# Clustered attention with a mixture of experts: a planner that lets VectorE and GpSimd exclude each other, selection's small operands in PSUM, and more experts in plain float32

## The chip, the cores and the metric

The kernel runs on one core of a Trainium2 chip. A core has five engines that work through their own queues of instructions, in order: PE (TensorE, the matmuls; its weight loads are listed apart as PEld), DVE (VectorE), ACT (ScalarE), POOL (GpSimd) and SP (SyncE, which here only issues transfers). SBUF is the working memory of 128 partitions, PSUM the small memory that matmuls write into. The metric is the time of one execution on the device, in microseconds (us); of several runs the median is given.

## The reference

Attention first, for 4 batches, 8 heads, 768 positions and 64 dimensions. Queries and keys are each assigned to the nearest of 16 centroids of their head, by cosine; a query only sees keys of its own cluster.

```python
q_assign = argmax(q_n @ c_n.T); k_assign = argmax(k_n @ c_n.T)
scores = where(q_assign == k_assign, q @ k.T / 8, -1e9)
attn = softmax(scores); x = (attn @ v)          # laid out as 3072 tokens of 512
```

Then a mixture of 8 experts over these 3072 tokens. Each token goes to its best expert; of an expert's tokens only the 80 with the highest gate are kept, the rows of all others are zero.

```python
e = argmax(x @ w_gate); g = softmax(x @ w_gate)[e]
for each expert: keep = the 80 tokens of it with the highest g
out[keep] = g[keep] * (relu(x[keep] @ w1[e]) @ w2[e])   # w1 512x1024, w2 1024x512
```

Everything is float32, and the clusters, the routing and the 80 kept tokens hang on exact comparisons, so the kernel computes to nearly full float32 precision.

## The kernel before

**One planned stream.** The whole program is laid out by a planner in the kernel's own Python. Work is written as lanes: generators that yield a `Step(engine, microseconds, ...)` ahead of the instructions of each step. `Flow.run` keeps a clock for each engine, takes the lanes' next steps, works out when each could start (its needs done, its buffer free, its engine free), picks the engine that can start first, and among its ready steps the one with the smallest due time `at`. The step's instructions are then emitted, and so stand in that order in the engine's queue. `CFG` holds the due times. So a step's cost, its due time or a new rule in `Flow.run` moves instructions on all engines; the data's dependencies stay guarded by semaphores whatever the order. For `alt` steps the planner also chooses between two engines.

**Attention** runs head by head, each in 6 blocks of 128 keys. Per block PE makes the scores (L562, L565, into `st`), ACT takes two exponentials (L584, L586: `pp` in float32 and `hh` in float16), POOL forms their difference `ll` (L593), and PE multiplies both parts with the values, which are split in a high and a low part (L601, `av`). For one block in five the float32 exponential stays in PSUM (`st`), and DVE forms `ll` instead. DVE also takes the row maxima of a first pass (L528 on PE, L530 on DVE) and normalises (L626 to L635). The tokens `x` are written to `xs` in HBM.

**The tail of attention** carries early work of the mixture. `early` starts in the last batch: 8 chunks of 512 KB of w1 (experts 0 and 1) are loaded into `raw` buffers, DVE takes their sums of squares (`stats`, L915), and `digits` cuts the gates `G` of the first 18 of 24 token tiles into digits: per level a shift (`di`, L694), a comparison with a ramp that gives `ge` (L696), a second shift (`pi`, L700) and a product with the routing one-hot `OH` that gives `pre` (L701); both results lie in the buffer `dug`. Up to now `di` and `pi` are in SBUF.

**Selection** finds each expert's 80th highest gate, digit by digit from the top, in five levels. In `select`, a level counts on PE how many candidates have a digit of at least each value (L747, into `q`), DVE compares the counts with what remains to be chosen (L781, `j`, `nf`), PE adds the chosen digit to the prefix in `nb` (L740), and DVE marks the candidates that still share the prefix (L790, `alive`). `digits` supplies the last batch's 6 tiles between. Then the threshold `thr`, the masks `M`, a scan `C` (L807), the slot of each kept token, and the row numbers `gi` (L850).

**The mixture** runs expert by expert on 80 tokens. POOL's queue gathers the rows (L1048) and scatters the results (L1172). ACT takes the rows' sums of squares, DVE makes a power of two of them (`power`, L878 to L881) and splits the scaled tokens in two float16 parts (L1065, L1066), PE turns them (L1085), and the hidden layer is 32 x 3 = 96 products of split tokens and split weights (L1114). A w1 chunk is split by ACT or DVE (high part, L1011 to L1016) and by DVE or POOL (low part, L1023, L1025). ReLU is ACT's, its low part `hl` DVE's (L1130). An expert in `native2` has its w2 multiplied as it was loaded, in plain float32: 8 products instead of 24 (L1142). The others' w2 is split in two parts on ACT or DVE (L1035, L1037) and POOL or DVE (L1041). An expert in `native1` would have its tokens and w1 multiplied in plain float32, 32 products instead of 96, without sums of squares, powers or splits. A raw chunk's buffer comes free once it is split; a plain one's when its products are done.

## Time and profile before

| | |
|---|---|
| median of 3 runs | 627.25 us (627.02 to 629.78) |
| the profiled execution | 624.93 us |
| its span, first to last instruction | 623.2 us |
| mean granted TensorE clock | 0.938 |
| busy in the span: PE / DVE / ACT / POOL | 552.7 / 501.1 / 474.4 / 441.3 us |
| moved | 114.26 MB |

The span covers everything from the first to the last instruction; 1.73 us lie around it. A row of a group gives line, engine, operation, tiles and shapes, the count after an x, then busy time, mean ns of one, and idle time of the engine just before it with what ended it. A row in order of time gives start and duration in us. A wait inside an instruction, as for a port, counts as its busy time. In the trace a float32 product shows as two weight loads and two matmuls. Line numbers are those of the kernel before.

### The profile page before, as it was taken

The page shows a single profiled execution, that of the slowest core. Times are in us where ns is not written, and L with a number is a line of the kernel's source. Part 1 is how long each engine was busy: PE and PEld are TensorE (multiplying, and loading weights), DVE is VectorE, ACT ScalarE, POOL GpSimd, SP SyncE. Part 2 cuts the span into 40 slices and gives each one's busy share as a digit, 9 for nine tenths or more (in the row PEclk, how much of TensorE's full clock was granted, in tenths as well). Part 3 has the DMA queues.
Part 4 walks back from the last instruction along what each step waited for, and adds up shares of the span by engine and source line. Part 5 has one row for each costly group of instructions (what it writes and reads, how often), then busy time and mean ns, then how long its engine had stood idle before and what let it go on. Part 6 is the DMA issues. An engine that isn't in the chain of part 4 may idle for free.

```text
span 623.2 us, 17162 instructions
## 1 busy us (share of the span) xinstructions
PE 552.7 (89%) x6781; PEld 448.7 (72%) x6781; DVE 501.1 (80%) x1070; ACT 474.4 (76%) x773; POOL 441.3 (71%) x276
## 2 busy tenths in 40 slices
PE   8999999999999999999999999998673638879795
PEld 7567877888888878888788888987562537565373
DVE  4868877888888888878878788799659848987992
ACT  7788788899899799889888987885449239746760
POOL 5359758799968689977688997776449215774775
PEclk9989999999999999999999999999775559989989
DMA  8688975499975489896448556492033773698200
GB/s 301 170 238 221 261 195 126 111 223 287 258 211 135 121 194 259 243 300 154 126 114 207 129 138 157 138 377 82 0 117 146 237 257 124 205 323 309 102 16 22
DMA packets 69776, 114.26 MB, mean 183 GB/s; under 512 B 7072, under 2 KB 38464, under 8 KB 69696
## 3 DMA queue, kind: packets, MB, share of 16 engines
q1 hardware_dynamic: 68672, 110.54, 61.7%
q0 software_dynamic: 1024, 2.62, 1.3%
q8 instruction: 54, 0.88, 0.6%
q14 instruction: 26, 0.21, 0.1%
HBM read 60.46 MB, written 13.89 MB: 119 GB/s over the span
## 4 chain that ended last, share of the span: by engine, by line
PE 53%; DVE 20%; DMA 9%; issue 6%; ACT 5%; POOL 5%; SPq 1%; POOLq 0%; ACTq 0%; DVEq 0%
PE av L601 15%; PE sm L528 11%; PE st L562 9%; PE st L565 8%; DMA raw<-in_w_dram 3%; DVE mx L530 2%; DVE w1p L1025 2%; DVE room L915 2%; POOL w1p L1023 2%; DVE dug L696 1%; PE misc L211 1%; ACT hh L586 1%; PE hp L1114 1%; DMA KAB<-hi 1%; DVE dug L701 1%
## 5 line engine op out<-in xcount | busy, mean ns | idle before, releaser
L593 POOL TENSOR_TENSOR ll<-pp,hh 128x768 f16<-128x768 f32 x154 | 255.1, 1669 | 78.0 <-ACT hh L586 38.9
L530 DVE TENSOR_REDUCE mx<-sm 128x1 f32<-128x384 f32 x384 | 201.7, 551 | 46.8 <-PE sm L528 44.2
L584 ACT ACTIVATE pp<-st 128x768 f32<-128x768 f32 x154 | 124.9, 811 | 42.3 <-PE st L565 37.8
L528 PE MATMUL sm<-KAB,QAB 80*128 80x384 f32 x384 | 141.3, 394 | 1.7 <-DVE mx L530 1.1
L601 PEld LDWEIGHTS <-hh 128*128 128x128 f16 x2304 | 121.8, 99 | 25.7 <-issue 15.1
L601 PE MATMUL av<-vh,ll 128*128 128x73 f16 x1152 | 135.6, 198 | 3.1 <-POOL ll L593 3.1
L601 PE MATMUL av<-vh,hh 128*128 128x73 f16 x1152 | 137.9, 200 | 0.0
L601 PE MATMUL av<-vl,hh 128*128 128x72 f16 x1152 | 136.7, 198 | 0.0
L586 ACT ACTIVATE hh<-st 128x768 f16<-128x768 f32 x154 | 124.6, 809 | 0.0
L601 PEld LDWEIGHTS <-ll 128*128 128x128 f16 x1152 | 113.5, 99 | 3.6 <-POOL ll L593 3.6
L562 PE MATMUL st<-QAB,KAB 128*128 128x384 f32 x384 | 105.2, 355 | 6.7 <-DVE ll L593 5.3
L565 PE MATMUL st<-QAB,KAB 81*128 81x384 f32 x384 | 100.5, 343 | 0.5 <-DMA QAB<-row 0.5
L528 PEld LDWEIGHTS sm<-KAB,QAB 80*128 80x128 f32 x384 | 70.1, 189 | 22.1 <-DVE mx L530 12.4
L562 PEld LDWEIGHTS st<-QAB,KAB 128*128 128x128 f32 x384 | 67.4, 193 | 12.0 <-DVE ll L593 5.2
L565 PEld LDWEIGHTS st<-QAB,KAB 81*128 81x128 f32 x384 | 71.1, 192 | 0.8 <-DMA QAB<-row 0.8
L1114 PE MATMUL hp<-xt,w1p 128*128 128x80 f16 x768 | 33.7, 213 | 6.2 <-POOL w1p L1023 6.1
L1048 POOL DMA_INDIRECT room<-xs,gi x8 | 16.2, 2020 | 31.7 <-DVE g L855 15.3
L593 DVE TENSOR_TENSOR ll<-st,hh 128x768 f16<-128x768 f32 x38 | 36.1, 949 | 2.6 <-ACT st L586 2.5
L1114 PEld LDWEIGHTS <-w1p 128*128 128x128 f16 x768 | 32.6, 108 | 7.5 <-POOL w1p L1023 6.5
L318 POOL TENSOR_TENSOR vl<-ldv,vh 128x512 f16<-128x512 f32 x24 | 27.1, 1128 | 11.6 <-ACT vh L316 11.6
L584 ACT ACTIVATE hh<-st 128x768 f16<-128x768 f32 x38 | 31.0, 817 | 4.2 <-PE st L565 3.9
L1023 POOL TENSOR_TENSOR w1p<-raw,w1p 128x1024 f16<-128x1024 f32 x12 | 27.8, 2332 | 5.0 <-ACT w1p L1012 4.9
(282 smaller groups left out, 988.0 us busy)
## 6 DMA issues: line engine op xcount, KB each, us to landing
raw<-in_w_dram SPq DMA_DIRECT2D x38, 512.0 KB
KAB<-hi SPq DMA_DIRECT2D x60, 192.0 KB
QAB<-hi SPq DMA_DIRECT2D x30, 384.0 KB
room<-in_w_dram SPq DMA_DIRECT2D x22, 512.0 KB
ldk<-in_kT_dram SPq DMA_DIRECT2D x16, 384.0 KB
ldq<-in_qT_dram SPq DMA_DIRECT2D x16, 384.0 KB
ldvt<-in_vT_dram SPq DMA_DIRECT2D x12, 512.0 KB
ldv<-in_v_dram SPq DMA_DIRECT2D x12, 512.0 KB
```

What stands on the lines that cost most here:

```text
L318: nc.gpsimd.tensor_tensor(lo, t[:, c], hi, op=ALU.subtract)
L528: nc.tensor.matmul(s, lhsT=qj, rhs=k[0:D + C, 0, f * HS:(f + 1) * HS], start=True, stop=True)
L530: nc.vector.tensor_reduce(mx[:, j, f:f + 1], s, axis=AX.X, op=ALU.max)
L562: nc.tensor.matmul(s[:, f, 0:HS], lhsT=k[:, 1, ks], rhs=q[:, 1, qs], start=True, stop=False)
L565: nc.tensor.matmul(s[:, f, 0:HS], lhsT=k[0:D + C + 1, 0, ks], rhs=q[0:D + C + 1, 0, qs], start=False, stop=True)
L584: nc.scalar.activation(order[0], s, AF.Exp, scale=float(D) ** -0.5)
L586: nc.scalar.activation(order[1], s, AF.Exp, scale=float(D) ** -0.5)
L593: eng.tensor_tensor(ll, pp, hh, op=ALU.subtract)
L601: mm = lambda out, l, r, **kw: nc.tensor.matmul(out, lhsT=l, rhs=r, skip_group_check=True, **{"start": False, "stop": False, **kw})
L1023: nc.gpsimd.tensor_tensor(t[:, 1], raw, t[:, 0], op=ALU.subtract)
L1048: nc.gpsimd.indirect_dma_start(out=xg[0:Mb], out_offset=None, in_=self.xs[:, :], in_offset=bass.IndirectOffsetOnAxis(ap=gi[0:Mb, e:e + 1], ...
L1114: nc.tensor.matmul(hp[:, f, :], lhsT=wt[:, a, fs], rhs=xt[:, x, k, :], start=(k == 0 and i == 0), stop=(k == K - 1 and i == 2))
```

## The change

- **The planner** learns that POOL's instructions and some DVE steps exclude each other. These steps get `two=True`: sums of squares, weight splits, the token split. Such a DVE step is planned to start only after the POOL step that began before it, and a POOL step after the last such DVE step. POOL's indirect transfers are outside the rule. Costs and due times are set anew.
- **Small operands in PSUM.** `di` and `pi` of `digits`, the scratch of `power`, `mx`, `ti`, `thr` and `pt` of `select`, and the scan's reset pattern `rst` move from SBUF into PSUM; counts, prefixes and scratch share banks. The prefix matmuls of the next level are issued ahead of its counts, not after them.
- **Token scaling** is cut in two steps, `factors` (the powers) and `tokens` (the split); the last gate arithmetic has one instruction less.
- **Plain float32**: w2 of experts 0, 2, 3, 4, 5 (before: 2, 3, 4) and w1 of expert 1 (before: none). Twelve of the remaining w1 chunks are now scaled for POOL's low part (before 14).

The new order at three places, rows as the program lists them (a product or a weight chunk each). First DVE in the tail of attention, up to one of the `ll` that DVE forms (`room_8070` takes the squares, which nobody reads, `wss` their sums). Before:

```order
L700 TENSOR_SCALAR pi<-G 128x18
L701 TENSOR_TENSOR dug<-OH,pi 128x144
L915 SCALAR_TENSOR_TENSOR room_8070,wss<-raw 128x1024
L694 TENSOR_SCALAR di<-G 128x18
L696 TENSOR_TENSOR dug<-di,K 128x558
L915 SCALAR_TENSOR_TENSOR room_8070,wss<-raw 128x1024
L700 TENSOR_SCALAR pi<-G 128x18
L701 TENSOR_TENSOR dug<-OH,pi 128x144
L915 SCALAR_TENSOR_TENSOR room_8070,wss<-raw 128x1024
L593 TENSOR_TENSOR ll<-st,hh 128x768
```

and now, where `misc` is a PSUM tile:

```order
L916 SCALAR_TENSOR_TENSOR room_8070,wss<-raw 128x1024
L923 TENSOR_REDUCE wss<-wss 128x1
L696 TENSOR_SCALAR misc<-G 128x18
L698 TENSOR_TENSOR dug<-misc,K 128x558
L702 TENSOR_SCALAR misc<-G 128x18
L703 TENSOR_TENSOR dug<-OH,misc 128x144
L696 TENSOR_SCALAR misc<-G 128x18
L698 TENSOR_TENSOR dug<-misc,K 128x558
L593 TENSOR_TENSOR ll<-st,hh 128x768
```

Seven sums of squares stand ahead of this `ll` before, counted from the first of them; four now, and all five levels' digits instead of four. Second, DVE in one level of selection, before:

```order
L694 TENSOR_SCALAR di<-G 128x6
L696 TENSOR_TENSOR dug<-di,K 128x186
L767 SCALAR_TENSOR_TENSOR j_9494<-j,q 8x31
L769 TENSOR_REDUCE mx<-j_9494 8x1
L771 TENSOR_SCALAR rem<-mx,rem 8x1
L700 TENSOR_SCALAR pi<-G 128x6
L701 TENSOR_TENSOR dug<-OH,pi 128x48
L1041 TENSOR_TENSOR w2p<-room_7987,w2p 128x1024
L781 TENSOR_SCALAR j,nf<-q,rem 8x31
L694 TENSOR_SCALAR di<-G 128x6
L696 TENSOR_TENSOR dug<-di,K 128x186
L790 SCALAR_TENSOR_TENSOR alive<-dug,nb 128x96 x2
```

and now (`dp` is a PSUM tile):

```order
L696 TENSOR_SCALAR dp<-G 128x6
L698 TENSOR_TENSOR dug<-dp,K 128x186
L781 TENSOR_SCALAR j,nf<-q,rem 8x31
L702 TENSOR_SCALAR dp<-G 128x6
L703 TENSOR_TENSOR dug<-OH,dp 128x48
L791 SCALAR_TENSOR_TENSOR alive<-dug,nb 128x96 x2
L696 TENSOR_SCALAR dp<-G 128x6
L698 TENSOR_TENSOR dug<-dp,K 128x186
L767 SCALAR_TENSOR_TENSOR j_9398<-j,q 8x31
L769 TENSOR_REDUCE q<-j_9398 8x1
```

The weight splits (L1016, L1025, L1037, L1041) that stood among the levels are gone from all five; they come after `gi`. Third, POOL's queue from the last of selection's tables to the first gathers, before and now:

```order
L715 TENSOR_TENSOR R<-OH,g_9317 128x192 x3
L1023 TENSOR_TENSOR w1p<-raw,w1p 128x1024
L1041 TENSOR_TENSOR w2p<-room_8070,w2p 128x1024
L1041 TENSOR_TENSOR w2p<-room_8225,w2p 128x1024
L1041 TENSOR_TENSOR w2p<-room_8301,w2p 128x1024
L1023 TENSOR_TENSOR w1p<-raw,w1p 128x1024 x4
L1048 DMA room_8301<-xs,gi 80x512
```

```order
L718 TENSOR_TENSOR R<-OH,g_9248 128x192 x3
L1022 TENSOR_TENSOR w1p<-raw,w1p 128x1024
L1040 TENSOR_TENSOR w2p<-room_8480,w2p 128x1024
L1040 TENSOR_TENSOR w2p<-room_8561,w2p 128x1024
L1040 TENSOR_TENSOR w2p<-room_8765,w2p 128x1024
L1040 TENSOR_TENSOR w2p<-raw,w2p 128x1024
L1047 DMA room_8301<-xs,gi 80x512
```

Eight weight splits stood ahead of the first gather, five do now.

The diff, cut to its core:

```diff
-           ... warm=48, nab=6, lag=3, share=(1, 5), raws=8, slots=(19, 5), native1=(),
-           native2=(2, 3, 4), ..., scaled=(3, 4, 5, 6, 7, 8, 11, 12, 13, 17, 20, 22, 24, 27),
+           ... warm=48, nab=6, lag=3, share=(1, 5), raws=8, slots=(19, 5), native1=(1,),
+           native2=(0, 2, 3, 4, 5), ..., scaled=(3, 4, 5, 6, 7, 11, 13, 14, 17, 19, 20, 21, 22, 24, 27, 29),
...
+        if t0:
+            dp = self.pss.tile([P, len(self.levels), 2, n], F32, name="dp", tag="pos")
...
-            di, pi = T("di"), T("pi")
+            di, pi = ((dp[:, l] if t0 else self.misc([P, 2, n])).bitcast(I32)[:, i] for i in range(2))
...
-        rst = w.tile([P, 2, E, NT], F16, name="rst")
+        rst = self.pss.tile([P, 2, E, NT], F32, name="rst")
+        nc.scalar.copy(rst, rs16)
...
+        def banks(l):
+            q, nb = ps.tile([E, 36], F32, name="q", bufs=2), ps.tile([P, 3 * E + NT], F32, name="nb", bufs=2)
+            if l == 0 or self.levels[l][0]:
+                nc.tensor.matmul(nb[:, 0:E], lhsT=self.ones[0:E], rhs=self.view["idl"][0:E, 0:E], start=True, stop=False)
+                for i, x in enumerate(nfs):
+                    nc.tensor.matmul(nb[:, 0:E], lhsT=x.broadcast_to([E, P]), rhs=ids[i], start=False, stop=False)
+            return q, nb
...
-    def power(self, out, ss, n):
-        ti = self.pre.tile([P, 3], I32, name="pw", bufs=6)
+    def power(self, out, bank, ss, n):
+        nc, ti = self.nc, bank.bitcast(I32)
...
+    def factors(self, u):
+        ss, bank = self.xss.pop(u), self.misc([P, 8])
+        self.power(bank[:, 4:6], bank, ss[0:Mb], Mb)
+        s = self.sx[u] = w.tile([P, 1], F32, name="sx", bufs=3)
+        nc.vector.tensor_copy(s[0:Mb], bank[0:Mb, 4:5])
...
-                    yield Step("pool", 2.32, alt=("dve", 1.15), key=("lo2", n), needs=[("hi2", n)], at=U * e + A["lo2"] + .1 * k)
+                    yield Step("pool", 2.32, alt=("dve", 1.2), two=True, key=("lo2", n), needs=[("hi2", n)], at=U * e + A["lo2"] + .1 * k)
...
+                    if eng == "dve" and step.two and self.pool[0] < start:
+                        start = max(start, self.pool[1])
+                    if eng == "pool" and not step.swdge:
+                        start = max(start, self.port)
...
+            if eng == "pool" and not step.swdge:
+                self.pool = start, done
+            if eng == "dve" and step.two:
+                self.port = done
```

More of the change, by code (lines that the diff above doesn't have):

```diff
@@ L734, in select @@
         alive, rem, nfs = [self.OH[:, 0:half], self.OH[:, half:]], float(cap), []
-        def prefix(last):
-            for i, x in enumerate(nfs if not last else nfs[-1:]):
-                k = len(nfs) - 1 if last else i
-                nc.tensor.matmul(nb, lhsT=x.broadcast_to([E, P]), rhs=ids[k], start=sh == 0, stop=last)
+        def banks(l):
[5 more added lines that the diff above has]
+            return q, nb
         for l, (sh, d0, ge, pre) in enumerate(self.levels):
@@ L782, in select @@
             nfs.append(nf)
-            yield Step("pe", .07)
-            prefix(True)
-            np_, nb_, nj = q[:, 0:nk], nb, nk
+            yield Step("pe", .18)
+            nc.tensor.matmul(nb[:, 0:E], lhsT=nf.broadcast_to([E, P]), rhs=ids[l], start=sh == 0, stop=True)
+            q_, nb_, nj = q, nb, nk
             if sh:
-                yield Step("dve", .33, needs=[("pre", l)])
+                more = .18 * (l + 2) if self.levels[l + 1][0] else .02
+                yield Step("dve", .43, also=("pe", more), needs=[("pre", l)])
                 alive = [w.tile([P, half, E], F16, name="alive", bufs=4) for _ in range(2)]
@@ L926, in totals @@
         self.tot = psum
-        nc.tensor.matmul(psum, lhsT=self.ones, rhs=ss[:, ss.shape[1] - 1:], start=True, stop=True)
+        nc.tensor.matmul(psum[:, 0:1], lhsT=self.ones, rhs=ss[:, ss.shape[1] - 1:], start=True, stop=True)
     def scale_w(self, e):
@@ L990, in early_stats @@
             for k in range(N1):
-                yield Step("dve", 1.14, needs=[("ld", 0, e * N1 + k)])
+                yield Step("dve", 1.14, needs=[("ld", 0, e * N1 + k)], two=True)
                 self.stats(e, k, "dve")
@@ L1224, in highs @@
                     needs = [("pw", e), ("ld", 0, n)] + ([("hid", last[e - A["a1"]], KF - HB)] if e >= A["a1"] else [])
[L1225 removed]
+                    yield Step("act", 2.1 if s else 1.05, alt=None if s else ("dve", .7), two=True, key=("hi1", n), needs=needs, room=("any", 1), at=U * e + A["hi1"] + .1 * k)
                     self.high1(e, k, flow.which, s)
@@ L1229, in highs @@
                     needs = [("ld", 1, n)] + ([("out", last[e - A["a2"]], KF - HB)] if e >= A["a2"] else [])
-                    yield Step("act", .96, alt=("dve", .68), key=("hi2", n), needs=needs, room=("any", 2), at=U * e + A["hi2"] + .1 * k)
+                    yield Step("act", .96, alt=("dve", .68), two=True, key=("hi2", n), needs=needs, room=("any", 2), at=U * e + A["hi2"] + .1 * k)
                     self.high2(e, k, flow.which)
@@ L1259, in rows @@
             if not n1:
-                yield Step("act", .62, needs=[("xg", i), *back(i, 2, "tp")], at=p, seq=True)
+                yield Step("act", .72, needs=[("xg", i), *back(i, 2, "tp")], at=p, seq=True)
                 self.norms(u)
-                yield Step("dve", 1.9, key=("xr", i), needs=[("slots", u[1])], at=p, seq=True)
+                yield Step("dve", 1.0, needs=[("slots", u[1])], at=p, seq=True, take="misc", give="misc")
+                self.factors(u)
+                yield Step("dve", 1.25, key=("xr", i), at=p, seq=True, two=True)
                 self.tokens(u)
@@ L1534, in Step @@
 def Step(eng, t, **more):
-    return SimpleNamespace(**{**dict(eng=eng, t=t, key=None, needs=(), at=None, late=0.0, rows=.5, early=False, alt=None, also=None, dma=(), take=None, give=None, kind=0, room=None, seq=False, swdge=0.0), **more})
+    return SimpleNamespace(**{**dict(eng=eng, t=t, key=None, needs=(), at=None, late=0.0, rows=.5, early=False, alt=None, also=None, dma=(), take=None, give=None, kind=0, room=None, seq=False, swdge=0.0, two=False), **more})
 class Lane:
```

106 lines of the change are left out of this document (47 added, 59 removed).

## The prediction

> **What bounds the kernel now.** Times are of the one profiled execution: 624.93 us for a span of 623.2 us, so 1.73 us lie around the span. The median of the three runs is 627.25 us, 2.32 us above it. I sum changes against the profiled execution and add 2.32 us at the end.
>
> I first cut the last third of the span by stage. The columns of this table of stretches are the stretch, its length, busy time and count of PE, PEld, DVE, ACT and POOL, the granted TensorE clock, the DMA share and GB/s.
>
> ```profile
> 408.90:441.80 32.90, 24.14 (x351) 21.15 (x347) 32.30 (x58) 18.74 (x28) 19.84 (x11) 0.97 0.49 184
> 441.80:457.80 16.00, 14.60 (x216) 13.42 (x216) 5.88 (x18) 8.77 (x12) 8.21 (x5) 0.84 0.00 1
> 457.80:461.20 3.40, 0.61 (x18) 0.49 (x18) 3.06 (x13) 0.21 (x1) 0.00 (x0) 0.89 0.02 6
> 461.20:501.40 40.20, 22.46 (x224) 18.63 (x224) 37.02 (x71) 25.47 (x35) 22.39 (x17) 0.50 0.63 214
> 501.40:512.90 11.50, 1.98 (x17) 1.72 (x18) 3.83 (x25) 3.37 (x7) 2.25 (x3) 0.50 0.81 276
> 512.90:618.00 105.10, 89.19 (x1045) 61.19 (x1042) 88.80 (x131) 66.63 (x98) 68.94 (x28) 0.96 0.48 162
> ```
>
> Read down the DVE column. In the tail of attention (first row) DVE has 32.3 of 32.9 us; in selection (fourth row) 37.0 of 40.2 us, while PE runs at clock 0.50. Only the mixture (sixth row) belongs to TensorE: 89.2 of 105.1 us. So DVE sets two stages and TensorE one.
>
> Next, what DVE does in them. Here is the tail in order of time (start, duration), with one row each of PE, ACT and POOL.
>
> ```profile
> 431.27 1.65 DVE L701 TENSOR_TENSOR dug<-OH,pi 128x144 f32<-128x144 f16 x1
> 435.44 1.60 DVE L694 TENSOR_SCALAR di<-G 128x18 int32<-128x18 int32 x1
> 437.07 2.12 DVE L696 TENSOR_TENSOR dug<-di,K 128x558 f16<-128x558 int32 x1
> 440.47 0.31 DVE L701 TENSOR_TENSOR dug<-OH,pi 128x144 f32<-128x144 f16 x1
> 441.83 0.95 DVE L593 TENSOR_TENSOR ll<-st,hh 128x768 f16<-128x768 f32 x1
> 442.91 0.74 DVE L696 TENSOR_TENSOR dug<-di,K 128x558 f16<-128x558 int32 x1
> 442.85 1.01 PE L562 MATMUL st<-QAB,KAB 128*128 128x384 f32 x2 [5.07 <-DVE ll L593]
> 434.02 0.91 ACT L586 ACTIVATE st<-st 128x768 f32<-128x768 f32 x1
> 429.43 9.17 POOL L593 TENSOR_TENSOR ll<-pp,hh 128x768 f16<-128x768 f32 x5 [5.86 <-PE misc L927]
> ```
>
> The same operation on the same shape takes 1.65 us at 431.27 and 0.31 us at 440.47 (L701), 2.12 us at 437.07 and 0.74 us at 442.91 (L696); the long ones start inside POOL's run of five instructions (429.43 to 438.60), the short ones after it. DVE waits, and the wait is booked as its busy time. The L593 behind them had its input from ACT (434.02) by about 434.9, started at 441.83, and PE stood 5.07 us for it.
>
> In selection the same, and here one row tells which DVE operations escape:
>
> ```profile
> 470.02 7.09 POOL L1041 TENSOR_TENSOR w2p<-room,w2p 128x1024 fp32r<-128x1024 f32 x3
> 470.05 0.40 DVE L790 SCALAR_TENSOR_TENSOR alive<-dug,nb 128x96 f16<-128x96 f32 x2
> 472.43 2.46 DVE L696 TENSOR_TENSOR dug<-di,K 128x186 f16<-128x186 int32 x1
> ```
>
> Both DVE rows lie inside POOL's 7.09 us. L790 reads `nb` from PSUM and does two instructions in 0.40 us; L696 reads two operands from SBUF and takes 2.46 us, about one POOL instruction (7.09 / 3 = 2.36).
>
> **The change, part by part.**
>
> *(a) Attention's tail.* Groups of DVE from 408.9 to 441.8 (busy, mean ns):
>
> ```profile
> L915 DVE SCALAR_TENSOR_TENSOR room<-raw 128x1024 f16<-128x1024 f32 x7 | 10.8, 1547 | 0.1
> L696 DVE TENSOR_TENSOR dug<-di,K 128x558 f16<-128x558 int32 (+1 forms) x4 | 4.2, 1059 | 0.1
> L701 DVE TENSOR_TENSOR dug<-OH,pi 128x144 f32<-128x144 f16 x4 | 4.0, 992 | 0.1
> L694 DVE TENSOR_SCALAR di<-G 128x18 int32<-128x18 int32 x4 | 2.7, 666 | 0.0
> ```
>
> L701's wait is 4.0 - 4 x 0.31 = 2.8 us. L694 cannot take more than L701's 0.31 alone, so at least 2.7 - 1.2 = 1.5 us of it is wait, and L696 waits 4.2 - 4 x 0.74 = 1.2 us. With small operands in PSUM these 5.5 us go. Expert 1 in plain float32 needs no sum of squares: three of the seven L915 ahead of the late L593 go, 3 x 1.55 = 4.6 us. One more digit step (0.9 us) now stands ahead of L593. DVE is thus 5.5 + 4.6 - 0.9 = 9.2 us earlier at L593. ACT's input caps what L593 itself gains at 441.83 - 434.9 = 6.9 us, unless the head before it also starts earlier; it does by the waits ahead of it, 1 to 3 us. Then POOL is next: five of its instructions took 9.17 us, and they must still run. I take 8.5 us, with 4 and 11 as the ends.
>
> *(b) Selection*, 461.20 to 501.40. Groups of DVE there:
>
> ```profile
> L696 DVE TENSOR_TENSOR dug<-di,K 128x186 f16<-128x186 int32 (+1 forms) x5 | 5.7, 1142 | 0.2
> L694 DVE TENSOR_SCALAR di<-G 128x6 int32<-128x6 int32 x5 | 5.7, 1135 | 0.0
> L701 DVE TENSOR_TENSOR dug<-OH,pi 128x48 f32<-128x48 f16 x4 | 4.7, 1164 | 0.1
> L1041 DVE TENSOR_TENSOR w2p<-room,w2p 128x1024 fp32r<-128x1024 f32 x2 | 4.4, 2198 | 0.0
> L1025 DVE SCALAR_TENSOR_TENSOR w1p<-raw,sw,w1p 128x1024 f16<-128x1024 f32 x3 | 3.8, 1270 | 0.0
> L700 DVE TENSOR_SCALAR pi<-G 128x6 int32<-128x6 int32 x4 | 2.5, 614 | 0.0
> ```
>
> L694 to L701 are 18.6 us for 18 instructions that take at most 0.31 to 0.4 us each when free, so some 13 us of it is wait. L1041 and L1025 (8.2 us) are weight work that the new order has no longer among the digits. They cannot all be subtracted, since some cover PE's turns; so I take the stage's length from its one undisturbed level, in the chain of waits:
>
> ```profile
> 490.55 0.42 DVE alive L790 x2
> 493.80 0.18 DVE ti L795
> 501.34 0.07 DVE gi L850
> 501.81 7.73 DMA raw<-in_w_dram
> ```
>
> From `alive` to the next result of `nb` is 493.80 - 490.55 = 3.25 us, and the rest to `gi` 7.54 us, with one L1025 in it that costs about 0.4 us. New stage: five levels of at most 3.25 = 16.3, then 7.1: 23.4 us instead of 40.2. The prefix matmuls now stand ahead of the counts on PE, and PSUM operands cost something: +0.5 us. Gain 16.3 us. No row shows a DVE operation that reads SBUF alone and writes PSUM under a busy POOL. If it waits as L694 does now, only the moved weight work is gained, 8 us; if all goes, 18.
>
> The Trainium skill sides with the high end. "SBUF — State Buffer", section "Who interferes with whom", says that a VectorE instruction with at most one SBUF input, outside the two-port modes, does not contend with GpSimd; "VectorE: DVE Perf Modes", section "Why PSUM operands drop a tier", says that any PSUM operand excludes those modes. L790 against L696 agrees; by the rule (b) would be about 18 us.
>
> *(c) From `gi` to the first hidden matmul*, 11.5 us now, of which 7.73 us wait for the gather behind weight loads. The order adds one weight split (1.27 us) between its two token steps. POOL must be through four `w2p` of 2.36 us ahead of the gather, which it is at about the new `gi`. +1.5 us; ends -2 and +4.
>
> *(d) The mixture.* PE's work, first the two lines alone in the sixth stretch (busy of PE, of PEld; L1114 hidden layers, L1142 outputs), then groups of it:
>
> ```profile
> 512.90:618.00 105.10, 33.71 (x768) 32.59 (x768) 0.96 0.48 162
> 512.90:618.00 105.10, 51.42 (x168) 23.96 (x168) 0.96 0.48 162
> L1142 PE MATMUL yp<-raw,hh 128*80 128x512 f32 x28 | 12.7, 594 | 0.0
> L1142 PE MATMUL yp<-room,hh 128*80 128x512 f32 x20 | 9.2, 598 | 0.0
> L1114 PE MATMUL hp<-xt,w1p 128*128 128x80 f16 x768 | 33.7, 213 | 6.2 <-POOL w1p L1023 6.1
> L1142 PE MATMUL yp<-w2p,hl 128*80 128x512 f32 x40 | 16.0, 399 | 4.1 <-DVE hl L1130 4.1
> L1500 PE MATMUL tot<-K,one 128*128 128x128 f16 x45 | 3.1, 228 | 0.0
> L927 PEld LDWEIGHTS tot<-wss,ones x12: 186/193/333, 499.9 to 591.1; 128*128 128x128 f32 x12
> ```
>
> A plain float32 w2 costs (12.7 + 9.2) / 3 = 7.3 us an expert, a split one (51.42 - 21.9) / 5 = 5.9 us: two more, +2.8 us. A split w1 costs 33.71 / 8 = 4.2 us. The plain one is 32 products, which the trace shows as two weight loads and two matmuls each, as it does L1142's (48 rows for 24 products): 64 pairs. No row has its shape. Low: by the columns, 21.9 / 48 x 80 / 512 = 0.071 us a pair, 4.6 us. High: by the slowest load in L927's row, 0.333 us (at half clock), 21 us. The weights have L927's shape, its median is 0.193 us, and loads overlap matmuls: I take 0.15 us, 9.6 us, +5.4 us. Dummies fall from 45 (3.1 us) to the 16 between these products: -2 us.
>
> Here a page speaks against what bounds it from below. "TensorE: Matmul & The Clock Gate", section "Weight-path perf modes — Fast Weight Load (FWL) and DoubleRow", says that the fast weight load, measured at about twice the speed, isn't available to FP32. The f16 pairs run at 33.71 / 768 = 0.044 us; at twice that an estimate by this page is 5.6 us, 4 us below mine.
>
> PE's work becomes 89.2 + 2.8 + 5.4 - 2.0 = 95.4 us. Its idle time is 105.1 - 89.2 = 15.9 us, of which 6.2 us are waits for POOL's w1 splits and 4.1 us for DVE's `hl`. POOL has fewer splits (12 and 8 for 14 and 9), DVE fewer waits; I take half, 8 us. New stage 103.4 us, -1.7; ends -10 (low w1, idle 5) and +13 (w1 at 15 us, idle as now). A cover is needed: if POOL keeps DVE waiting in the large splits, which stay in SBUF, the 8 us return.
>
> Sum: -8.5 - 16.3 + 1.5 - 1.7 = -25.0 us, 599.9 us for such an execution, 602 us beside the median shown. The 5 us from the last matmul to the end stay.
>
> **Rivals.** *1. TensorE takes the mixture's gain and more*: w1 at 15 us and idle time undiminished, +13 us, 615 us. For it: PE already has 89 of 105 us. Against: half of its waits name DVE or POOL. *2. More is freed than I count*: 11 us in (a), 18 in (b), mixture -5: 32 us or so, 594 us and below. For it: PE's waits in the tail; against: POOL's own pace there. *3. The change doesn't do what it says*: results in PSUM leave the wait, because the source is still read through the contested path. Then (b) gains 8, (a) 5: 614 us; with rival 1, 628 us. Against it: L790. *4. Slower: raw chunks are held.* Plain float32 weights keep their buffers until their matmuls have run, 24 chunks instead of 12. A load then waits for PE, and PE for load and split: at 276 GB/s a 512 KB chunk takes 1.9 us, four of them 7.6 us, and their splits 4 x 1.27 = 5.1 us, 12.7 us an expert. Two such turns uncovered (25 us) undo the gain, three give 640 us. Against it: DMA is busy only 0.48 of the mixture, so there is room to load ahead.
>
> **How the numbers follow.** The forecast (594 to 611) has 0.55; rival 1 and 3 alone (611 to 622) 0.22; rival 2 (below 594) 0.13; rivals 1 and 3 together, no change (within 0.5%, 624 to 630, about what a measurement of this kernel tells apart) 0.05; rival 4 0.05. Faster 0.90, same 0.05, slower 0.05. The range from 587 to 618 leaves out the upper end of the third case, the low tail and the last two.
>
> **What would show it.** (a) PE waits under 2 us for L593 in the tail, and the stage that ends at 457.8 ends near 449. (b) The digit operations have means under 0.5 us, and `OH` to `gi` takes 22 to 25 us. (c) The first hidden matmul starts 12 to 15 us after `gi`. (d) PE is busy over 94 us in the mixture, with idle time below 12 us. I am wrong in mechanism if the digit operations still have means over 1 us, and in size if the mixture is 10 us longer or shorter than 103.4 us.

## The result and the profile after

The change takes 586.34 us (median of four runs, 583.0 to 588.15) against 627.13 us (four runs, 625.9 to 629.78): ratio 0.9338, 95% interval 0.9283 to 0.9393, so 40.8 us less. The forecast was 602 us. The profiled execution took 588.15 us for a span of 586.0 us. Of all executions below, one of `jit_fill` took 836.28 us at a mean granted clock of 0.555 and is not used.

The stretches of the changed kernel, from a step of attention that both profiles have (`L635` at 404.53 us before, 405.51 us now) to the end of the last output; columns as in the prediction's first table:

```profile
405.51:447.76 42.25, 38.83 (x583) 33.53 (x581) 29.48 (x68) 30.87 (x44) 31.43 (x18) 1.00 0.47 170
447.76:451.24 3.48, 0.00 (x0) 0.00 (x0) 3.13 (x14) 0.21 (x1) 0.00 (x0) 1.00 0.05 15
451.24:474.22 22.98, 19.21 (x224) 16.30 (x224) 13.92 (x65) 17.93 (x26) 15.01 (x14) 0.55 0.84 273
474.22:487.26 13.04, 2.40 (x24) 2.22 (x24) 9.85 (x20) 8.38 (x13) 6.42 (x4) 0.56 0.91 290
487.26:580.78 93.52, 89.57 (x964) 59.11 (x962) 65.23 (x112) 60.22 (x94) 54.77 (x27) 0.97 0.60 199
```

| stage | before us | after us | change | forecast |
|---|---|---|---|---|
| end of attention (last `den`) | 457.83 | 447.76 | -10.1 | -8.5 |
| selection, first digit to `gi` | 40.2 | 23.0 | -17.2 | -16.3 |
| `gi` to first hidden matmul | 11.5 | 13.0 | +1.5 | +1.5 |
| mixture | 105.1 | 93.5 | -11.6 | -1.7 |
| whole span | 623.2 | 586.0 | -37.2 | -25.0 |

(Before with the prediction's rounded boundaries; after with the rows above.) Ten of the twelve microseconds that the sum missed are in the mixture. The medians differ by 4 us more than the two profiled executions do (624.93 and 588.15 us): that of before lay 2.2 us under its median, that of the change 1.8 us over.

The late L593 in attention's tail now follows digit steps that don't wait, although sums of squares (L916) beside them still do. In order of time, first POOL's run of five instructions, then DVE beside it:

```profile
427.75 9.23 POOL L593 TENSOR_TENSOR ll<-pp,hh 128x768 f16<-128x768 f32 x5 [5.34 <-ACT hh L586]
428.29 2.24 DVE L916 SCALAR_TENSOR_TENSOR room<-raw 128x1024 f16<-128x1024 f32 x1
432.18 0.18 DVE L696 TENSOR_SCALAR misc<-G 128x18 int32<-128x18 int32 x1
432.39 0.74 DVE L698 TENSOR_TENSOR dug<-misc,K 128x558 f16<-128x558 int32 x1
433.30 0.96 DVE L593 TENSOR_TENSOR ll<-st,hh 128x768 f16<-128x768 f32 x1 [0.17 <-ACT st L586]
```

The L593 on DVE now waits 0.17 us for ACT; before it came 7 us after ACT. PE's waits in the tail that name an L593 are down to 0.7 us in all. In selection, the digit groups of DVE (L696, L698 and L703 were L694, L696 and L701 before):

```profile
L698 DVE TENSOR_TENSOR dug<-dp,K 128x186 f16<-128x186 int32 x4 | 1.4, 352 | 0.1
L703 DVE TENSOR_TENSOR dug<-OH,dp 128x48 f32<-128x48 f16 x4 | 0.8, 204 | 0.1
L696 DVE TENSOR_SCALAR dp<-G 128x6 int32<-128x6 int32 x5 | 0.8, 154 | 0.0
```

Means of 0.15 to 0.35 us in place of 1.1 to 1.2. In the mixture, first what PE waited for (total us, times, longest) before, then now, then groups of PE and of DVE now:

```profile
PE hp L1114 <- POOL w1p L1023: 6.1, 3, 2.8
PE yp L1142 <- DVE hl L1130: 4.1, 2, 2.1
PE yp L1142 <- POOL w2p L1041: 2.3, 3, 1.1
PE tp L1085 <- DVE room L1066: 1.2, 3, 0.5
PE tp L1085 <- DVE room L1065: 1.1, 2, 0.8
PE tot L927 <- DVE wss L922: 0.9, 1, 0.9
```

```profile
PE yp L1146 <- DVE hl L1134: 3.2, 1, 3.2
PE tp L1089 <- DVE room L1072: 0.5, 1, 0.5
PE tp L1089 <- DVE room L1071: 0.3, 1, 0.3
```

```profile
L1118 PE MATMUL hp<-xt,w1p 128*128 128x80 f16 x672 | 26.6, 205 | 0.0
L1111 PE MATMUL hp<-xt,raw 128*128 128x80 f32 x64 | 8.4, 278 | 0.0
...
L1024 DVE SCALAR_TENSOR_TENSOR w1p<-raw,sw,w1p 128x1024 f16<-128x1024 f32 x8 | 12.1, 1514 | 0.0
L1040 DVE TENSOR_TENSOR w2p<-raw,w2p 128x1024 fp32r<-128x1024 f32 x3 | 5.7, 1889 | 0.0
L1040 DVE TENSOR_TENSOR w2p<-room,w2p 128x1024 fp32r<-128x1024 f32 x1 | 4.1, 4096 | 0.0
```

Before, all but 0.1 us of PE's 15.8 us of idle time named POOL (8.4 us) or DVE (7.3 us). PE's waits for POOL are gone, and 4.0 us in all are left, all for DVE. DVE's own waits are not gone: a free L1040 takes 1.21 us, one took 4.10.

### The profile page after: what moved, and what is told of

The parts are those of the page before. It is cut to its first block, busy times and chain, and to the rows that moved or that the text cites. A ratio compares the mean times of both kernels' runs of the same rounds, so it can differ in the third digit from the quotient of the medians.

```text
span 586.0 us, 16832 instructions
## 1 busy us (share of the span) xinstructions
PE 544.2 (93%) x6641; PEld 438.3 (75%) x6641; DVE 449.2 (77%) x1027; ACT 464.8 (79%) x766; POOL 423.0 (72%) x273
## 5 line engine op out<-in xcount | busy, mean ns | idle before, releaser
L593 POOL TENSOR_TENSOR ll<-pp,hh 128x768 f16<-128x768 f32 x154 | 254.4, 1665 | 68.4 <-ACT hh L586 36.2
L601 PEld LDWEIGHTS <-hh 128*128 128x128 f16 x2304 | 120.5, 98 | 25.7 <-issue 14.7
L562 PE MATMUL st<-QAB,KAB 128*128 128x384 f32 x384 | 104.8, 354 | 2.3 <-ACT hh L586 2.0
L593 DVE TENSOR_TENSOR ll<-st,hh 128x768 f16<-128x768 f32 x38 | 36.1, 950 | 2.1 <-ACT st L586 2.0
L1022 POOL TENSOR_TENSOR w1p<-raw,w1p 128x1024 f16<-128x1024 f32 x10 | 26.1, 2606 | 14.5 <-ACT w1p L1011 12.5
L367 POOL TENSOR_TENSOR ldk<-ldk,hi 128x768 fp32r<-128x768 f32 x15 | 27.4, 1828 | 5.2 <-ACT hi L365 2.8
L586 ACT ACTIVATE st<-st 128x768 f32<-128x768 f32 x38 | 30.7, 807 | 0.0
L394 POOL TENSOR_TENSOR ldq<-ldq,hi 128x768 fp32r<-128x768 f32 x15 | 27.4, 1827 | 2.6 <-DVE vss L270 1.8
## 6 DMA issues: line engine op xcount, KB each, us to landing
KAB<-hi SPq DMA_DIRECT2D x60, 192.0 KB
```

Of the source, the lines that this page charges most:

```text
L367: nc.gpsimd.tensor_tensor(lo, t, hi.bitcast(F32), op=ALU.subtract)
L394: nc.gpsimd.tensor_tensor(lo, t, hi.bitcast(F32), op=ALU.subtract)
L562: nc.tensor.matmul(s[:, f, 0:HS], lhsT=k[:, 1, ks], rhs=q[:, 1, qs], start=True, stop=False)
L586: nc.scalar.activation(order[1], s, AF.Exp, scale=float(D) ** -0.5)
L593: eng.tensor_tensor(ll, pp, hh, op=ALU.subtract)
L601: mm = lambda out, l, r, **kw: nc.tensor.matmul(out, lhsT=l, rhs=r, skip_group_check=True, **{"start": False, "stop": False, **kw})
```

## The experiments

Every kernel below runs the same program up to the step L635, and its profiled executions reach it between 404.5 and 409.7 us. Stages are therefore counted from that mark (and by exact events, so that some of before differ by up to 0.4 us from those above): tail (mark to the last `den`), selection, `gi` to the first hidden matmul, mixture, and all of it to the end. Times in us; the ratio is to the kernel before in the same session.

| kernel | median | ratio, 95% | tail | sel. | to hid. | mixture | mark to end |
|---|---|---|---|---|---|---|---|
| before | 627.13 | 1 | 53.3 | 40.0 | 11.9 | 104.8 | 218.6 |
| the change | 586.34 | 0.934 [0.928, 0.939] | 42.2 | 23.0 | 13.0 | 93.5 | 180.5 |
| split_experts | 609.44 | 0.972 [0.967, 0.977] | 45.5 | 24.8 | 16.2 | 106.2 | 201.3 |
| float32_only | 601.11 | 0.959 [0.954, 0.964] | 51.3 | 29.7 | 9.2 | 94.2 | 193.1 |
| sel_sbuf | 597.56 | 0.956 [0.951, 0.961] | 52.0 | 25.9 | 10.5 | 92.3 | 189.3 |
| tail_psum | 590.05 | 0.942 [0.936, 0.947] | 42.2 | 25.5 | 11.3 | 92.9 | 180.5 |
| pow_sbuf | 588.18 | 0.941 [0.935, 0.946] | 42.3 | 23.2 | 12.2 | 92.8 | 179.1 |
| sets_before | 608.68 | 0.968 [0.964, 0.972] | 44.8 | 23.0 | 17.9 | 109.9 | 204.2 |
| due_before | 593.42 | 0.945 [0.942, 0.949] | 42.3 | 24.4 | 16.1 | 94.5 | 186.0 |
| split_w1 | 605.17 | 0.967 [0.961, 0.974] | 44.8 | 23.0 | 16.6 | 103.5 | 196.7 |
| w2_three | 602.75 | 0.963 [0.957, 0.968] | 42.3 | 22.7 | 18.4 | 100.0 | 192.0 |
| rule_off | 601.61 | 0.962 [0.956, 0.968] | 44.5 | 23.0 | 13.2 | 103.3 | 192.8 |
| jit_st | 599.55 | 0.954 [0.949, 0.959] | 42.3 | 23.0 | 13.5 | 105.2 | 192.7 |
| ahead2 | 596.49 | 0.951 [0.945, 0.957] | 42.2 | 23.2 | 12.8 | 102.3 | 189.3 |
| joined | 593.24 | 0.947 [0.943, 0.950] | 42.3 | 23.2 | 11.2 | 98.9 | 184.3 |
| fill | 582.21 | 0.927 [0.921, 0.933] | 42.3 | 23.2 | 10.0 | 92.4 | 176.5 |
| jit_fill2 | 590.36 | 0.943 [0.933, 0.954] | 42.2 | 23.2 | 10.0 | 97.4 | 181.5 |
| before_fill | 599.39 | 0.954 [0.947, 0.961] | 54.6 | 33.4 | 11.3 | 84.4 | 192.3 |

### The two halves of the change, each alone

`split_experts` is the change with the experts and mixture settings of before (the planner's `bias` for `alt` steps, 1.2 against 1.25, among them); `float32_only` is the kernel before with those of the change.

```diff
# split_experts, in the change
-native1=(1,), native2=(0, 2, 3, 4, 5), scaled=..., mix=... of the change
+native1=(), native2=(2, 3, 4), scaled=..., mix=... of before
# float32_only, in the kernel before: the same lines the other way
```

> The changed kernel with the experts of the kernel before: w2 of experts 2, 3, 4 alone in plain float32, no plain w1, and that kernel's choice of chunks and due times; small operands in PSUM and the planning with the exclusion stay. Theory A (plain float32 takes split work off POOL, DVE and ACT, and that empties TensorE's waits in the mixture): mixture 100 to 105 us, with TensorE idle 10 us or more in it; selection within 2 us of 23.0; 593 to 600 us. Rival B (PSUM and the exclusion in the plan did it, the plain experts change nothing): mixture below 96 us, time within 3 us of 586. Rival C (the plain experts cost TensorE more than they free): below 584 us.

> The kernel before with only the changed sets: w2 of five experts and w1 of expert 1 in plain float32, the chunks and due times that belong to them; small operands in SBUF, the plan without the exclusion. Theory A (the parts add up): the tail of attention shorter by 2 to 5 us (three sums of squares fewer), selection within 4 us of 40.2, mixture 95 to 99 us; 612 to 620 us against 627. Rival B (plain experts help only when DVE no longer waits for POOL): mixture at 102 us or more, 622 to 630 us.

Measured: 609.4 and 601.1 us. The mixtures:

```profile
496.71:602.88 106.17, 89.25 (x1001) 62.34 (x1001) 93.99 (x138) 67.08 (x96) 70.69 (x31) 0.89 0.48 160
```

```profile
500.19:594.40 94.21, 89.20 (x963) 57.59 (x960) 66.39 (x113) 57.97 (x89) 51.81 (x27) 0.98 0.58 194
```

The mixture's gain belongs to the plain experts with their settings: 94.2 us with them and nothing else, 106.2 us with all but them. They also shorten selection (40.0 to 29.7). PSUM and the plan shorten the tail and selection. From the mark the plain experts alone are worth 25.6 us, PSUM and the plan alone 17.3, both together 38.1: 4.7 us can be had by either. The plain experts were worth more than any theory had of them: 612 to 620 us expected with them alone, 601 measured; 593 to 600 expected without them, 609 measured.

### Where the small operands lie

Three kernels with the change's order on every engine; only the place of tiles differs. `sel_sbuf`: digits and selection in SBUF. `tail_psum`: the same, but the digits inside attention's tail stay in PSUM. `pow_sbuf`: only the operands of the power-of-two factors in SBUF.

```diff
# tail_psum; sel_sbuf has also di, pi of the early digits in w.tile; pow_sbuf only the last pair
-            dp = self.pss.tile([P, len(self.levels), 2, n], F32, name="dp", tag="pos")
+            dp = w.tile([P, len(self.levels), 2, n], F32, name="dp")
... (rst, mx, ti, thr and pt in the same way)
-        nc, ti = self.nc, bank.bitcast(I32)
+        nc, ti = self.nc, self.pre.tile([P, 4], F32, name="pw", bufs=6).bitcast(I32)
```

> The changed kernel with the small operands of the digits and of selection (the digit, the prefix, the reset mask of the scan, the thresholds, the positions) in SBUF again. Every engine has the same instructions in the same order as in the changed kernel; only where these tiles lie differs. Theory A (a DVE instruction with two SBUF operands waits for POOL's large instruction, one with an operand in PSUM does not): the digit operations have means near 1 us again under POOL (0.15 to 0.35 now), the tail of attention is longer by 3 to 6 us (its 5.5 us of waits in the kernel before), selection by 8 to 16 us (23.0 now, 40.2 before), the mixture within 2 us of 93.5; 597 to 606 us in all against 586. Rival B (the new order holds the gain: no large weight work among the digits): under 3 us more, below 590 us.

> The changed kernel with only the digit operations inside attention's tail in PSUM; the small operands of selection itself are in SBUF again, same order everywhere. With all of them in SBUF the time was 597.6 us, 11 us above the change: 9 in the tail, 2.9 in selection, and 2.5 us less from the row numbers to the first hidden matmul. Theory G (the weight loads, not DVE, set the time from the first digits to the first hidden matmul): selection 26, the stage behind it 10.5 us, 36 in sum as in the change; 585 to 588 us. My forecast's view (PSUM in selection is worth most of 16 us): 590 us or more.

> The changed kernel with only the small operands of the power-of-two factors (of expert weights and of tokens) in SBUF again, same instructions, same order. Theory A: the fourth operation of each factor (1.33 us mean in the kernel before, 0.16 now) and the two after it wait for POOL again, some 11 factors by 1 to 2 us of DVE; as DVE is busy 65 of the 93.5 us of the mixture, only a part reaches TensorE: mixture 95 to 99 us, 588 to 592 us in all. Rival B (DVE's slack hides it all): mixture within 1 us of 93.5 and the time within 1 us of 586. Rival C (all of the mixture's gain over my forecast comes from here): mixture at 101 us or more.

`sel_sbuf` loses 9.8 us in the tail, where the digit steps (L702, L703) wait again for POOL's run; POOL and DVE in order of time:

```profile
428.48 7.55 POOL L593 TENSOR_TENSOR ll<-pp,hh 128x768 f16<-128x768 f32 x4 [5.86 <-ACT hh L586]
428.59 1.61 DVE L702 TENSOR_SCALAR di<-G 128x18 int32<-128x18 int32 x1
430.24 1.70 DVE L703 TENSOR_TENSOR dug<-OH,di 128x144 f32<-128x144 f16 x1
```

In selection it loses only 2.9 us, and wins 2.5 back before the first hidden matmul. `tail_psum` confirms it: 180.5 us from the mark, as the change. Its median (590.05) is above what was expected, but its execution reached the mark 1.8 us later and the intervals overlap. Selection with its operands in SBUF and the stage behind it:

```profile
452.95:478.42 25.47, 18.64 (x204) 15.72 (x204) 18.54 (x66) 18.33 (x26) 15.21 (x14) 0.54 0.85 278
478.42:489.71 11.29, 2.40 (x23) 2.21 (x24) 9.85 (x20) 7.78 (x12) 6.42 (x4) 0.50 0.81 265
```

36.8 us in sum against 36.0. So PSUM in selection is worth under 1 us in this order. One reason is that the digit steps are as good as done when POOL's first weight split starts; the last of them and that split, in `tail_psum`:

```profile
460.75 0.35 DVE L698 TENSOR_TENSOR dug<-dp,K 128x186 f16<-128x186 int32 x1
460.96 2.13 POOL L1022 TENSOR_TENSOR w1p<-raw,w1p 128x1024 f16<-128x1024 f32 x1 [3.84 <-ACT w1p L1011]
```

Under POOL's splits only L777 (1.5 us) and L806 (2.5 us) still wait, and one L696 (0.85 us) under POOL's small products before. The other reason, as far as the rows tell, is that the weight side ends the two stages. ACT must do a sum of squares (L918) and a split ahead of the first token step, and its chunk arrives 25.2 us after the first digit in the change (476.49 - 451.24) and 25.6 us in `sel_sbuf` (485.76 - 460.11), whether or not `gi` is ready by then:

```profile
476.49 1.06 ACT L918 ACTIVATE room<-raw 128x1024 f16<-128x1024 f32 x1 [1.66 <-DMA raw<-in_w_dram]
```

```profile
485.76 1.06 ACT L918 ACTIVATE room<-raw 128x1024 f16<-128x1024 f32 x1 [0.25 <-DMA raw<-in_w_dram]
```

`pow_sbuf` can't be told from the change (mixture 92.8 for 93.5), as rival B said: about 4 us of waits come back to DVE's small steps, and PE doesn't notice. The time of `sel_sbuf` was as theory A expected, but with 9.8 us in the tail and 2.9 in selection where 3 to 6 and 8 to 16 had stood.

### Which experts, and which due times

```diff
# split_w1                # w2_three                      # sets_before: both sets of before
-native1=(1,)             -native2=(0, 2, 3, 4, 5)        # due_before: the change's sets,
+native1=()               +native2=(2, 3, 4)              #   scaled and mix of before
```

> The changed kernel with w1 of expert 1 split again into f16 parts (its four sums of squares, its scale and its eight chunk steps return); five plain w2 stay. With both sets of before the time was 609.4 us, 23 us above the change. Theory A (the gain goes with the split work taken off DVE, ACT and POOL: per expert, w1 has four sums of squares more than w2, so it is worth more than one of the two w2): 594 to 600 us, most of it between the digits and the first hidden matmul and in the tail, where expert 1 is split; mixture 93 to 97 us. Rival B (plain w1 costs TensorE 8.4 us for 3.8 and gives as much as it takes): within 3 us of 586. Rival C (it holds nearly the whole gain): 603 us or more.

> The changed kernel with w2 of experts 0 and 5 split again (experts 2, 3, 4 stay plain), w1 of expert 1 plain. Theory A: eight casts of ACT or DVE (about 1 us each) and eight subtractions of POOL (2.36 us, 19 us) return; POOL is busy 55 of 93.5 us in the mixture and TensorE gets 2.8 us less work, so the mixture is 95 to 100 us and the time 590 to 597 us. Rival B (TensorE's work decides): 583 to 586 us. Rival C (nearly the whole gain): 603 us or more.

> The changed kernel with the plain experts of the kernel before (w2 of experts 2, 3, 4; no w1) but its own due times and chosen chunks. With the due times of before as well, the time was 609.4 us and the mixture 106.2. Theory A (plain experts make the gain): mixture 102 us or more, 603 us or more. Theory D (the due times make it): mixture 97 us or less, 592 us or less. In between both have a part.

> The changed kernel (its plain experts, small operands in PSUM, exclusion in the plan) with the due times and the chosen chunks of the mixture of the kernel before. What is open: three kernels that differ from the change in one part of the mixture all have a mixture of 100 to 106 us, and one of them (a limit on queued loads) has all of the split work of the change. Theory A (plain experts make the gain, whatever the due times): mixture 93 to 97 us, 585 to 591 us. Theory D (the due times of the change fit its plan, and the gain is only there with them): mixture 100 us or more, 594 us or more.

With split experts the due times of the change gain nothing (204.2 us from the mark, 201.3 with those of before); with plain ones they are worth 5.5 us (186.0 to 180.5), of which 1.0 lies in the mixture (94.5, 93.5) and 3.1 between `gi` and the first hidden matmul. So the sets make most of the gain, as theory A had it. How it is shared between w1 and w2 stays open: `split_w1` and `w2_three` lie above theory A's ranges (605.2 and 602.8 us), giving back one set costs 16.2 or 11.5 us from the mark, giving back both 23.8, and the next group shows that a plan with the same work can lose 12. Over all plans (fills left aside) the mixture takes 92.3 to 105.2 us with the plain sets and 104.8 to 109.9 us with those of before, so the direction stands, but a single difference is uncertain by several us.

### The plan with the same work

`rule_off` ignores the flag of the exclusion; `jit_st` has one due time 0.5 us later; `ahead2` limits queued loads; `joined` plans the first token step in one piece. With the order, a few of the steps that may go to either engine change theirs (DVE takes 4 sums of squares in the change, 4 to 9 in these).

```diff
# rule_off
-if eng == "dve" and step.two and self.pool[0] < start:
+if False and eng == "dve" and step.two and self.pool[0] < start:      (and the rule for POOL)
# jit_st                  # ahead2                         # joined
-st=-20.3                 -spare=-0.08                     -Step("dve", 1.0, ...), Step("dve", 1.25, two=True)
+st=-19.8                 +spare=-0.08, ahead=2.0          +Step("dve", 2.25, ...) for the first expert
```

> The changed kernel, planned without the exclusion of VectorE and GpSimd (the flag of the steps is ignored); small operands in PSUM and plain experts as in the change. The order of the large weight work moves, nothing else. Theory A (the exclusion in the plan is worth little, since the waits of the small operands are gone by PSUM and TensorE's by the plain experts): 585 to 590 us, the mixture within 2 us of 93.5. Rival B (the plan is what keeps large DVE work from standing under POOL): means of the large DVE splits up, mixture 96 to 102 us, 590 to 596 us.

> The changed kernel with one due time of the mixture (that of the sums of squares of w1) 0.5 us later; nothing else. About two dozen steps on each engine change their place. It measures how far a plan moves the time when neither work nor operands change. Theory A: within 3 us of 586. Theory D: up to 10 us above it, all of it in the mixture, as TensorE waits at one or two places for a step that has slipped behind others in its queue.

> The changed kernel, planned so that a weight load is issued only when the planned DMA backlog is under 2 us (no limit now). The first gather then waits for less queued data. If the backlog ahead of the gather sets the 13.0 us from the row numbers to the first hidden matmul: 10 to 11.5 us there, mixture within 1 us, 583 to 585 us. If ACT and the stalled DVE step behind it set them, or the loads come late in the mixture: 586 to 590 us.

> The changed kernel with the token step of the first expert planned as one step, so that no weight split (1.7 us in the change) stands on DVE between the factors of its tokens and their scaling. From the row numbers to the first hidden matmul 11 to 11.5 us in place of 13.0. If the rest of the plan stays as good, 584.5 us; if the reordering that it brings costs as much as the other plans that were moved, 590 us or more.

All four lose 3.8 to 12.3 us from the mark, nearly all in the mixture, more than was expected of three of them, and none beats the change. `joined` does what it was meant to at its place (11.2 for 13.0 us) and loses 5.4 us behind it. The clearest place is in `rule_off`; DVE, then PE:

```profile
552.96 7.88 DVE L1040 TENSOR_TENSOR w2p<-room,w2p 128x1024 fp32r<-128x1024 f32 x3
560.76 0.14 DVE L923 TENSOR_REDUCE wss<-wss 128x1 f32<-128x4 f32 x1
560.96 0.59 PE L928 MATMUL tot<-wss,ones 128*128 128x1 f32 x2 [8.87 <-DVE wss L923]
```

Three splits that a plan without the exclusion counts at 1.2 us each take 7.88 us beside POOL's. A small sum (L923) is queued behind them, and TensorE, in order, stands 8.87 us before a matmul of 0.59 us; output matmuls follow right behind it. But `jit_st` has the rule and loses as much, and `float32_only` has no rule and loses nothing in the mixture. So the rule isn't shown to be worth 12 us: a plan without it can be good, one with it bad. The three longest of TensorE's waits in the mixture of `jit_st`:

```profile
PE yp L1146 <- DVE hl L1134: 6.0, 1, 6.0
PE yp L1146 <- ACT hh L1127: 4.0, 1, 4.0
PE hp L1118 <- POOL w1p L1022: 2.5, 2, 2.0
```

### Is it DVE's wait for POOL?

In `fill`, `jit_fill` and `before_fill` each large subtraction of POOL in the weight splits is a fill of the same tile (the low parts are left out), in the orders of the change, `jit_st` and the kernel before.

```diff
-            nc.gpsimd.tensor_tensor(t[:, 1], raw, t[:, 0], op=ALU.subtract)
+            nc.gpsimd.memset(t[:, 1], 0.0)                                    (low2 in the same way)
```

> The changed kernel in which each large subtraction of POOL in the weight splits is a fill of the same tile with zeros: the low parts of those weights are left out, the order on every engine is the same. DVE then has no POOL instruction with two SBUF operands beside its weight work. Theory E (DVE's waits under POOL's splits, 18 us of its large weight operations in the mixture, are what the plan has to hide): those waits fall below 4 us; the mixture is 89 to 92 us, as TensorE's work is 89.6; 580 to 585 us. Rival F (order alone): DVE's waits may fall, the mixture stays within 1 us of 93.5.

> The kernel before with the same fills in place of POOL's subtractions of weights (low parts left out). Theory E: the waits of its digit operations in selection (about 13 us of DVE's busy time) and of the factors go without PSUM; selection 40 to 28 us or less, mixture 104.8 to 94-99 us; POOL's splits of attention (the softmax residuals) are not touched, so the tail keeps its waits (457.8 within 2 us). 600 to 608 us. Rival F: selection above 35 us and mixture above 101 us, 618 us or more.

> The kernel with one due time 0.5 us later (599.55 us, mixture 105.2) with the same fills in place of POOL's subtractions (the low parts of those weights are left out). Theory E: the two plans come together, mixture 90 to 94 us, at most 3 us from that of the fill in the changed kernel's order, 581 to 588 us. Rival F (the order itself costs the 12 us, by steps queued behind others on in-order engines): mixture still 100 us or more, 594 us or more.

> The kernel with one due time 0.5 us later and fills in place of POOL's weight subtractions (low parts left out), profiled once more. Theory E (the 12 us between the two plans are DVE's waits under POOL): mixture 90 to 94 us, as in the fill of the changed kernel (92.4). Rival F (order): 100 us or more. Its earlier times, 589 us against 582 us, lie between: half of it then.

The mixture of `before_fill`, then of `fill`, then of `jit_fill2` (the kernel `jit_fill` run once more; its 587.77 and 592.96 us agree with the 584.9 to 590.98 us of `jit_fill`):

```profile
508.73:593.18 84.45, 83.70 (x1042) 58.99 (x1040) 66.64 (x130) 65.69 (x97) 37.64 (x28) 0.98 0.57 201
```

```profile
487.65:580.02 92.37, 90.66 (x964) 60.59 (x962) 51.99 (x112) 60.44 (x94) 30.28 (x27) 0.96 0.60 208
```

```profile
488.61:585.96 97.35, 91.34 (x964) 60.64 (x962) 55.64 (x113) 60.42 (x93) 26.86 (x27) 0.95 0.57 196
```

`before_fill` is the run that explains most. With split experts and no POOL subtraction beside them, the mixture takes 84.4 us and TensorE is busy 83.7 of it, 0.7 us short of all. The kernel before took 104.8 us for the same matmuls: 20 us of its mixture went with POOL's subtractions. A fill also takes POOL less time (it is busy 37.6 us for 68.9), so this doesn't tell POOL's own lateness from DVE's waits under POOL.

With the plain experts TensorE is busy 90.7 us (`fill`), 7 more, and the change's mixture is within 3 us of that. Not all of the 7 is work, since the granted clock differs. In `fill` it is 0.50 from 499.0 to 505.8, and the same four products of plain w1 take

```profile
499.40 1.09 PE L1114 MATMUL hp<-xt,raw 128*128 128x80 f32 x4
509.48 0.62 PE L1114 MATMUL hp<-xt,raw 128*128 128x80 f32 x4
```

Split hidden products start 67 ns apart in such stretches and 36 ns apart outside. The ten kernels with the change's sets of experts and chunks and the same 964 matmul records are busy 88.4 to 92.7 us in the mixture; less half of the busy time at clock 0.50, an estimate of the time at full clock, all ten have 86.7 to 87.7 us. The same estimate gives 81.8 us for `before_fill`. The plain experts thus cost TensorE 5 to 6 us, and of what the mixture takes beyond that, 23.0 us before and 6.6 us in the change (93.5 less 86.9), 16 us are gone.

`fill` wins 3.0 us more between `gi` and the first hidden matmul, so POOL's splits are part of what holds the weight side there, and only 1.1 us in the mixture, although the waits of DVE's large steps there fall from 18.2 to 4.3 us. In the change's order these waits are hardly on the path. Between the two plans 12.2 us become 5.0 (176.5 and 181.5 from the mark): 7 of the 12 us come with POOL's subtractions. The other 5 lie in the mixture, where PE is idle 6.0 us in `jit_fill2` and 1.7 in `fill`; the order is one cause, but fills still hold some steps there (five L1015, 0.74 us each when free, take 9.7 us for 4.3 in `fill`), and the two are not separated. What theory E foresaw for the kernel before came true, and more (84.4 us where 94 to 99 had stood); it also covers up to somewhat over half of the scatter between plans. Its selection (33.4 us for 28 or less) did not come true; the last section shows why.

## Why the prediction was right and wrong

**Direction and the first three stages.** (a) Forecast -8.5, measured -10.1 (-11.1 from the mark). PSUM is its cause (`sel_sbuf`: +9.8 without it), more than the 5.5 us of waits I gave it. The 4.6 us of sums of squares were not a gain of their own: `float32_only`, without three of them, is 2.0 us shorter, partly since a digit step (L700, 1.60 us) then waited where they had stood. As an addition to PSUM they did pay (`split_w1` has 44.8, the change 42.2). Both signs that were named came true (0.7 us of PE's waits for L593; 447.8 for near 449). The sum was nearly right; two of its terms were not independent.

(b) Forecast -16.3, measured -17.2; both rows that were named came true (means under 0.5 us; 23.2 us from `OH` to `gi` for 22 to 25). But that is luck. The cause that I gave, PSUM, doesn't carry it: `tail_psum` with selection in SBUF has 25.5 us, and the 2.5 us come back before the first hidden matmul. Where the weight work stands is the likely carrier: DVE's splits are no longer among the digits, so that these end about when POOL's splits begin, and need no PSUM to be quick. No run puts that work back and keeps PSUM, so this is argued from rows. Nor is it shown what moved it: `float32_only` still has three of DVE's weight steps in selection (29.7 us); `rule_off` and `split_experts` have none (23.0 and 24.8), so neither the exclusion in the plan nor the plain experts are needed for it.

I had priced the moved work at 8 us, as the low end; all of the change but PSUM was worth 14.5 there (40.0 to 25.5). My rival 3 (PSUM doesn't cut the wait) fell: the waits are cut where POOL runs. The rule cited there from the Trainium skill, "SBUF — State Buffer", section "Who interferes with whom", agrees with the tail, where L703 takes 0.30 us inside POOL's run in the change and 1.70 us in `sel_sbuf`; what it says of a wait doesn't say whether the wait is on the path.

(c) Forecast +1.5, measured +1.5. The weight side sets it, as the forecast took it to, and the added split is in it: `joined`, without that split in its place, has 11.2 us for 13.0. How far the stage also undoes gains ahead of it I had not seen.

**The mixture, forecast -1.7, measured -11.6.** The forecast's 103.4 us were 95.4 us of PE and 8 us of idle time; measured were 89.6 and 3.9. The sign in (d) that PE is busy over 94 us did not come, the one on its idle time did. The added work was right: +6.2 forecast, +5 to +6 by the estimate at full clock. Plain w1 took 8.4 us against my 9.6 (0.132 us a pair against 0.040 for split products). The estimate of 5.6 us by the Trainium skill, "TensorE: Matmul & The Clock Gate", section "Weight-path perf modes — Fast Weight Load (FWL) and DoubleRow", was further off; the loads alone agree with its factor of two (192 ns against 102 for f16).

The step that failed is "PE's work becomes 89.2 + ...": I read PE's busy time as its work. `before_fill` does the same matmuls with 83.7 us busy, so 5.2 us of the busy time (88.9 by exact events) were not work. About 2.4 of them go with the granted clock, which is 0.50 for 8.7 us of the mixture before and for 3.9 in `before_fill`; two of these stretches (3.4 us each, at 549.2 and 593.6) begin within 1 us after a wait of PE, but other waits as long have none behind them, so their cause isn't shown. The hidden layers alone go from 33.7 to 30.7 us. The other 2.8 us, beside 14 waits of PE for 2, are not taken apart. The second step that failed is "I take half, 8 us" for the idle time of 15.9. Rival 1 has it that half of PE's waits name DVE or POOL; nearly all did (15.7 us), and 3.9 were left. Both errors are one: what late splits cost PE was counted too small.

What I left out altogether is how much hangs on the plan. Four orders of nearly the same work lie 3.8 to 12.3 us above the change. My range for the mixture (-10 to +13) was wider, but I had no such scatter in mind. The due times had been fitted to the changed plan, and I had counted those as neutral.

**Rivals.** Rival 2 (more is freed than I count, 594 us and below) is what happened, at 0.13, with 586 us: (a) and (b) came near its 11 and 18, and the mixture gave more than twice its 5. Rival 1 (TensorE takes the gain) was wrong in both its terms: plain w1 took 8.4 us and not 15, and the idle time fell by 12. Rival 4 (raw chunks held) shows in no wait: PE's three waits in the mixture name no DMA. The last 4 us of the miss are the profiled execution: I added 2.3 us for the median, and that of the change lies 1.8 us below its profile.

## What to carry to other kernels

Busy time of an engine is not yet its work: here the same matmuls were busy 88.9 us in one kernel and 83.7 in another, and about half of the difference lay in stretches with a granted clock of 0.50. Read the clock of each stretch beside the busy time. A run in which the feeder's work is made trivial, in the same order, gives a better floor and tells at once what removing that work can bring. A wait that is removed only counts as far as the next thing in line allows; sum the stage with the one behind it. And when a planner sets the order, compare several plans of the same work before a difference of a few per cent is laid to one of its parts.

## What the runs showed that was not expected

A wait of DVE under POOL isn't always one POOL instruction long. In `before_fill` one digit operation (0.16 us when free) lasted until the end of a whole run of POOL, small products and then eight fills without a gap between them:

```profile
466.85 8.52 DVE L694 TENSOR_SCALAR di<-G 128x6 int32<-128x6 int32 x1
```

```profile
466.44 1.81 POOL L715 TENSOR_TENSOR R<-OH,g 128x192 f16<-128x192 f16 x3
467.99 1.11 POOL L1023 MEMSET w1p<- 128x1024 f16 x1
469.03 2.74 POOL L1042 MEMSET w2p<- 128x1024 f32 x3
471.71 3.63 POOL L1023 MEMSET w1p<- 128x1024 f16 x4
```

So fills on POOL, which read nothing, hold such a step as well, and selection's 33.4 us in that kernel contain it. And the waits of DVE's large steps in the mixture did not fall with the change. As busy time less count times the shortest duration of each form they are some 12.5 us before and 18.2 now, while those of the small steps went from 13.9 to 0.2. They stand less in TensorE's way: of PE's waits 7.3 us named DVE before and 4.0 now, and `fill` takes 14 of the 18.2 us away for 1.1 us of the mixture.
